# A fixed table of order and engines in place of a list scheduler, in an attention, FFT and feed-forward kernel

## The chip, the cores and the metric

The kernel runs on one core of a Trainium2 chip. The metric is the device time in microseconds of one execution; below 5 us (0.5%) two kernels can't be told apart here. A core has TensorE (PE in the rows, its weight loads PEld), VectorE (DVE), ScalarE (ACT), GpSimd (POOL) and SyncE (SP), which issues nearly all DMAs. Each engine runs its own queue strictly in order, and an instruction whose input isn't there holds up everything behind it on that engine.

## The reference

```python
def reference(**kwargs):
    ...
    attn_out = _attn_ref(**attn_kwargs)      # sliding window of 64, 8 heads of 64
    B, H, S, D = attn_out.shape              # 8, 8, 576, 64
    x = np.ascontiguousarray(attn_out.transpose(0, 2, 1, 3)).reshape(B, S, H * D)
    return _moe_ref(x=x, **moe_kwargs)

def _moe_ref(x, w_ch1, w_ch2):
    X = np.fft.fft(x, axis=1)
    X = np.fft.fft(X, axis=2)
    u = x + np.real(X).astype(np.float32)
    ...
    un = (u - mu) / np.sqrt(var + 1e-06)
    ch = np.maximum(un @ w_ch1, 0.0) @ w_ch2     # 512 x 2048 and 2048 x 512
    return (u + ch).astype(np.float32)
```

Attention over 8 batches of 576 positions, a two-dimensional Fourier transform of its output whose real part is added to it, a normalisation, and a feed-forward net of 2048 hidden units with a residual. The two weight matrices arrive as 64-bit floats.

## The kernel before

**Tiles.** The 4608 positions are 36 tiles of 128 (T0 to T35; nine tiles are a pair of batches). A tile's attention is: load k, q, v (L434); bring k and q into head-major form (L471 for T0 to T12, DMA transposes later); scores (`psc`, L573 or L578); masking and row maximum on VectorE (L595); exponential on ScalarE (L603); transposing the probabilities (`pp`, L614) and copying them out of PSUM; times v (`pa`, L657); division on VectorE (L663 to L667); a radix-4 step for the transform (`y`, L414) and its transposition (`py`, L748). When a batch's tiles are done, `fft` does the rest of its transform: folds and sums on VectorE or GpSimd (L414, L832), splitting each into two f16 halves (`fs`, `hs`), two stages of matmuls (`pg` L888, `pz` L922), and a mix that goes through DRAM (`md`, `mt`). `norm_tile` adds and normalises, giving `uhl`.

**Feed-forward.** 18 chunks of two tiles, c0 to c17. In each, 16 steps `one(f)` (`ph`, L1208, fed by the first weights) and 16 steps `second(f)` (`po`, L1189, fed by the second). Two `one` steps share a PSUM bank; ScalarE (L1217) and then VectorE (L1220) turn it into `hh`, which two `second` steps read. There are two such banks and two `hh` buffers. c0 is the plain case (L1214) in f32; the others are three f16 passes over split weights. The feed-forward work fills TensorE wherever attention and transform leave it free.

**Weights.** 32 pieces of 512 KB (`weight_piece`): 16 of the first matrix (x0, g0 to g15) and 16 of the second (x1), in alternating fours. Each is loaded by SP (L1088), converted by three VectorE steps (L1097, L1102, L1109), and squared on ScalarE (L1115) for a scale. After the last piece of a matrix its scale is known, and `weight_split` (L1162 and a copy) makes the f16 halves for c1 on. Step `one(f)` of c0 needs four converted pieces:

```python
bws = [Bw[0][4 * (f // 4) + kc + at] for kc in range(4)]
op("PE", 1.73 if plain else 1.31, 1e6 + 32 * c + 2 * f, lambda f=f, one=one: one(f), [Bu[c], *bws], [bph])
```

so f12 to f15 need x0 g12 to g15.

**Order.** All 2900 operations are registered with `plan.op` (engine, planned duration, priority, reads, writes; `alt` names a second engine) and numbered as they come. `Plan.order` (L199) is a list scheduler over planned times: it repeatedly picks, of all engines, the operation that can start first, by priority where two tie, and lets an engine wait a little for a more urgent one (`PATIENT`). Of an operation with two engines it takes the second when that finishes sooner by a margin:

```python
sooner = max(free[e2], s2) + d2 + o.margin < max(free[e1], s1) + d1
...
key = (st, o.prio, o.idx)
```

The instructions are then issued in that order (L1278 on, under `manual_schedule`), so the list fixes each engine's queue and SP's queue of DMAs. Where the planner sees TensorE idle before the feed-forward starts, it puts in warm-up matmuls (L1284). An elementwise step on GpSimd is cut in pieces (`both`, L410):

```python
w = out.shape[1] // n if eng is nc.gpsimd else out.shape[1]
for k in range(0, out.shape[1], w):
    eng.tensor_tensor(out=out[:, k : k + w], in0=in0[:, k : k + w], in1=in1[:, k : k + w], op=al)
```

**Numbers that the prediction uses.** Tile T9: 673 scores, 674 and 678 masking of its two head groups, 675 and 679 exponentials, 676 and 680 `pp`, 682 and 684 `pa`. T10: 698 scores. Pieces x0 g12 to g15: conversions 132 to 134, 137 to 139, 142 to 144, 147 to 149. Transform of batch 1: folds 586 and 587, sums and splits 588 to 607, matmul stage 608 and 611. c0: `one(12)` is 397, `second(8)` to `second(11)` are 395, 396, 400, 401. Loads of T4: 271 (k), 272 (q), 273 (v); of T5: 487 to 489; loads of x0 g2, g3 and x1 g0: 21, 26, 31.

Of the kernel before, what the change touches and what calls it, by code (L numbers as in the profile page):

```python
# [53 lines left out]
YS = 32.0  # L54
PASSES = ((0, 0), (0, 1), (1, 0))
ONE = ((0, 0),)


D0, D2, DO1, DO2 = (0, 65), (65, 64), (129, 128), (257, 128)
# [73 lines left out]
class Plan:  # L133
# [3 lines left out]

    SEM = {"PE": 0.22, "DVE": 0.06, "ACT": 0.06, "POOL": 0.08, "DMA": 0.0}
    MARGIN = 0.4
    PATIENT = {"DVE": 0.25, "ACT": 0.5, "POOL": 0.75, "DMA": 0}  # L140
    SELF = {"PE": 0.05, "DVE": 0.02, "ACT": 0.02, "POOL": 0.03, "DMA": 0.0}

    FIXED = {"PE": 0.0, "DVE": 0.1, "ACT": 0.1, "POOL": 0.06, "DMA": 0.0}
# [52 lines left out]
            t += span  # L196
        return t

    def order(self):  # L199
        busy = {}  # L200
        engs = sorted({e for o in self.ops for e in o.durs})
        free = {e: 0.0 for e in engs}
        avail = {e: [] for e in engs}
        slots = {r: [0.0] * n for r, n in self.rings.items()}
        for o in self.ops:
            o.wait, o.ready = len(o.deps), 0.0
            for d in o.deps:
                d.outs.append(o)
        for o in self.ops:
            if not o.wait:  # L210
                for e in o.durs:
                    avail[e].append(o)
        line = {r: [] for r in self.fifo}
        for o in self.ops:
            for b in o.allocs:
                if b.ring in line:
                    line[b.ring].append(((o.prio, o.idx), o))
        for r in line:
            line[r] = [o for _, o in sorted(line[r], key=lambda x: x[0])][::-1]
        port = 0.0  # L220
        res = []
        n = len(self.ops)
        while len(res) < n:
            best = None
            for e in engs:
                t0 = free[e]
                pick, ahead = None, []
                for o in avail[e]:
                    r = o.ready
                    need = {}  # L230
                    for b in o.allocs:
                        need[b.ring] = need.get(b.ring, 0) + 1
                    ok = True
                    for ring, k in need.items():
                        if len(slots[ring]) < k or (ring in line and line[ring][-1] is not o):
                            ok = False
                            break
                        r = max(r, sorted(slots[ring])[k - 1])
                    if not ok:
                        continue  # L240
                    st = max(t0, r, port) if e == "POOL" or e == "DVE" and o.port else max(t0, r)
                    if len(o.durs) > 1:
                        (e1, d1), (e2, d2) = o.durs.items()
                        s1, s2 = (max(port, r) if x == "POOL" or x == "DVE" and o.port else r for x in (e1, e2))
                        sooner = max(free[e2], s2) + d2 + o.margin < max(free[e1], s1) + d1
                        if e != (e2 if sooner else e1):
                            continue
                    key = (st, o.prio, o.idx)
                    ahead.append((o.prio, key, o))
                    if pick is None or key < pick[0]:  # L250
                        pick = (key, o)
                if pick and e in self.PATIENT:

                    most = pick[0][0] + self.PATIENT[e] * pick[1].durs[e]
                    for pr, key, o in ahead:
                        if pr < pick[1].prio and key[0] < most and (pr, key) < (pick[1].prio, pick[0]):
                            pick = (key, o)
                if pick and (best is None or pick[0] < best[0]):
                    best = (*pick, e)
            if best is None:  # L260
                raise RuntimeError("the rings are too small for this order")
            (st, _, _), o, o.eng = best
            o.dur = o.durs[o.eng]
            for e in o.durs:
                avail[e].remove(o)
            gap = st - free[o.eng]
            self.gaps.append(gap)
            end = st + o.dur
            if o.eng == "PE":
                if gap > WARM[0] and o.prio < 1e6:  # L270
                    self.pe_time(busy, free["PE"], (gap - WARM[1]) / 2)
                end = self.pe_time(busy, st, o.dur)
            free[o.eng] = end
            if o.eng == "POOL" or o.eng == "DVE" and o.port:
                port = end
            done = end + o.lat
            for b in o.allocs:
                s_ = sorted(slots[b.ring])
                slots[b.ring] = s_[1:]
                if b.ring in line:  # L280
                    line[b.ring].pop()
            for b in o.bufs:
                b.left -= 1
                b.free_at = max(b.free_at, done + self.SEM[o.eng])
                if b.ring and b.left == 0:
                    slots[b.ring].append(b.free_at)
            for x in o.outs:
                x.wait -= 1
                late = x.slack * self.LATE[o.eng] if "PE" in x.durs else 0.0
                x.ready = max(x.ready, done + (self.SEM if o.eng not in x.durs or o.lat else self.SELF)[o.eng] + late)  # L290
                if not x.wait:
                    for e in x.durs:
                        avail[e].append(x)
            res.append((st, o))
        self.span = max(free.values())
        self.times = [st for st, _ in res]
        return [o for _, o in res]
# [3 lines left out]
def attn_fft_ffn_kernel(ctx: ExitStack, tc: tile.TileContext, q, k, v, w1, w2, gidx, dft_d, dft_s, mask, out):  # L301
# [14 lines left out]
    plan = Plan(RINGS, ("kq", "pr", "pt", "xu", "y", "yT", "tail", "xe", "r3", "fh", "g", "mp", "f1", "f2", "hh"))  # L316
# [754 lines left out]
    osc = cp.tile([P, 1], F32, name="osc")  # L1071

    def weight_piece(x, g, order):

        w, more = {}, order % 7 - 4 if order % 7 > 3 else None
# [41 lines left out]
        bj, bf = Buf("un"), Bw[x][g + 1]  # L1117
        bw = [Buf("big")] if more is None else Bfl[2 * more : 2 * more + 2]
        op("DMA", 1.75, W_DMA + W_DMA_STEP * order, load, writes=[*bw, Bwl], lat=2.5)
        pr = W_CONV + W_STEP * order  # L1120
        op("DVE", 0.34, pr, lambda: conv(0), bw, [bf])
        op("DVE", 0.6, pr - 0.1, lambda: conv(1), bw, [bf])
        op("DVE", 0.6, pr - 0.2, lambda: conv(2), bw, [bf])
        op("ACT", 0.72, W_SQ + W_STEP * order, square, [bf], [bj, Bssq[x]])

    def weight_scale(x, prio):
# [126 lines left out]
    for T in range(NTT):  # L1253
# [5 lines left out]
        pb, n = divmod(T, NT)  # L1259
# [16 lines left out]
    warm = bank("f1", "warm", (P, 2, CH))[:, 0]  # L1276
    early = True
    with tc.manual_schedule():  # L1278
        for o, gap in zip(plan.order(), plan.gaps):
            early = early and o.prio < 1e6  # L1280
            if early and o.eng == "PE" and gap > WARM[0]:

                for _ in range(int((gap - WARM[1]) / 0.21)):
                    nc.tensor.matmul(warm, wide[:, 0:P], wide, start=True, stop=True)  # L1284
            if len(o.durs) > 1:
                o.fn({"DVE": nc.vector, "POOL": nc.gpsimd, "ACT": nc.scalar}[o.eng])
            else:
                o.fn()
# [27 lines left out]
```

## Time and profile before

| what | value |
|---|---|
| median of 3 runs | 1000.35 us (998.46 to 1002.23) |
| profiled execution | 1000.41 us; span from first to last instruction 998.6 us |
| TensorE busy | 964.4 us (97%) |
| VectorE, ScalarE, GpSimd busy | 655.8, 394.2, 254.3 us |
| granted TensorE clock, mean | 0.989 |
| DMA | 123.08 MB |

A busy time is a union: overlapping instructions count once. TensorE's warm-up matmuls count as busy. "1.00" in a clock column is 2.4 GHz, "0.50" is 1.2 GHz. A wait is named by the instruction that ended it.

### The profile page before, as it was taken

How to read it: one execution, taken by the hardware profiler on the slowest of the kernel's cores; microseconds unless marked ns; L12 is line 12 of the kernel's file. 1: busy time of each engine (PE TensorE's matmuls, PEld its weight loads, DVE VectorE, ACT ScalarE, POOL GpSimd, SP SyncE). 2: the span in 40 equal slices, each digit the busy share in tenths (PEclk: the TensorE clock that was granted, in tenths of full speed). 3: DMA queues.
4: the chain of work that ended last, by engine and by line, in shares of the span. 5: the costliest groups of instructions: out<-in, count | busy, mean ns of one | idle time of the engine just before them, and what ended most of it. 6: DMA issues, size and time to landing. Idle time of an engine off the chain costs nothing.

```text
span 998.6 us, 22725 instructions
## 1 busy us (share of the span) xinstructions
PE 964.4 (97%) x8984; PEld 676.3 (68%) x8984; DVE 655.8 (66%) x1846; ACT 394.2 (39%) x893; POOL 254.3 (25%) x500
## 2 busy tenths in 40 slices
PE   7789969999999999999999999999999999999998
PEld 5576638767676667666676667766676677666664
DVE  5699998987875777775885678665867464511111
ACT  5564646762553444344442344233523121211010
POOL 0011100345245521252215254342404101400000
PEclk9899989999999999999999999999999999999999
DMA  9987663435965876888866777568636302410000
GB/s 195 233 216 214 186 167 119 99 67 119 173 156 132 165 153 141 158 168 174 155 124 154 130 150 135 116 133 165 111 86 120 75 1 68 74 32 22 1 22 21
DMA packets 309066, 123.08 MB, mean 123 GB/s; under 512 B 291096, under 2 KB 291224, under 8 KB 308960
## 3 DMA queue, kind: packets, MB, share of 16 engines
q1 hardware_dynamic: 306240, 112.72, 52.2%
q0 software_dynamic: 2720, 8.92, 3.4%
q8 instruction: 70, 1.15, 0.5%
q14 instruction: 36, 0.29, 0.1%
HBM read 54.99 MB, written 14.17 MB: 69 GB/s over the span
## 4 chain that ended last, share of the span: by engine, by line
PE 79%; DMA 8%; DVE 7%; POOL 2%; ACT 1%; SPq 1%; issue 1%; DVEq 0%; ACTq 0%; POOLq 0%
PE ph L1208 33%; PE po L1189 32%; PE pa L657 3%; DMA mt<-md,gix 3%; PE pz L922 3%; PE pg L888 2%; PE psc L578 2%; DMA kn<-in_k 1%; DMA pt<-flex 1%; DMA md<-mp 1%; POOL flex L414 1%; PE pp L614 1%; PE psc L573 1%; DMA qn<-in_q 1%; PE py L748 1%
## 5 line engine op out<-in xcount | busy, mean ns | idle before, releaser
L1208 PE MATMUL ph<-uhl,w0s 128*128 128x256 f16 (+1 forms) x3384 | 425.8, 277 | 0.3 <-DVE hh L1220 0.3
L1189 PE MATMUL po<-w1s,hh 128*128 128x512 f16 (+1 forms) x1696 | 426.0, 388 | 0.0
L1208 PEld LDWEIGHTS <-w0s 128*128 128x128 f16 x3264 | 316.5, 98 | 83.1 <-issue 1.9
L1189 PEld LDWEIGHTS <-hh 128*128 128x128 f16 x1632 | 155.7, 98 | 138.0
L1220 DVE SCALAR_TENSOR_TENSOR hh<-ph,hh 128x512 f16<-128x512 f32 x136 | 93.7, 689 | 156.7 <-ACT hh L1217 156.5
L1217 ACT ACTIVATE hh<-ph 128x512 f16<-128x512 f32 x136 | 81.0, 595 | 283.6 <-PE po L1189 212.1
L603 ACT ACTIVATE pr<-pr,nm 128x128 f32<-128x128 f32 x288 | 91.1, 390 | 26.8 <-DVE nm L595 26.7
L595 DVE CUSTOM_DVE_ANT_0 pr<-psc,mskb 128x128 f32<-128x128 f32 x288 | 65.8, 284 | 16.0 <-PE psc L573 11.4
L414 POOL TENSOR_TENSOR up<-un,up 128x128 f16<-128x128 f32 x128 | 55.4, 461 | 69.4 <-ACT up L404 69.4
L414 POOL TENSOR_TENSOR flex<-pr,flex 128x128 f16<-128x128 f32 x92 | 44.9, 516 | 96.9 <-ACT flex L404 79.3
L996 POOL DMA_INDIRECT mt<-md,gix x34 | 35.7, 1051 | 111.6 <-DMA md<-mp 103.5
L1020 POOL TENSOR_TENSOR rs<-mv,mhalf 128x1 f32<-128x1 f32 x36 | 23.2, 644 | 133.2 <-DVE mv L1016 126.7
L414 POOL TENSOR_TENSOR flex<-qn,flex 128x128 f16<-128x128 f32 x88 | 42.6, 518 | 47.4 <-ACT flex L404 34.8
L657 PE MATMUL pa<-ve,pt 128*64 128x65 f16 (+1 forms) x760 | 43.5, 206 | 3.6 <-DMA pt<-flex 2.3
L657 PE MATMUL pa<-va,pt 128*64 128x65 f16 (+1 forms) x760 | 43.6, 207 | 0.0
L1243 DVE SCALAR_TENSOR_TENSOR xu<-po,osc,xu 128x512 f32<-128x512 f32 x34 | 23.9, 745 | 22.6 <-PE po L1189 22.6
L404 ACT CAST up<-un 128x512 f16<-128x512 f32 x34 | 21.0, 616 | 43.7 <-DMA uhl<-up 14.4
L404 ACT CAST flex<-pr 128x512 f16<-128x512 f32 x40 | 24.6, 616 | 25.4 <-DMA pt<-flex 25.3
L667 DVE TENSOR_TENSOR xu<-pa,rc 128x256 f32<-128x256 f32 x72 | 30.6, 425 | 3.1 <-DMA out<-xu 0.7
L657 PEld LDWEIGHTS <-pt 128*64 128x64 f16 x1104 | 21.1, 111 | 16.7 <-issue 12.2
L922 PE MATMUL pz<-g,ds__75 97*96 97x257 f16 (+3 forms) x240 | 29.1, 273 | 1.0 <-DVE g L898 0.7
L614 PE MATMUL pp<-ident,pr 128*128 128x128 f32 x104 | 19.1, 299 | 9.9 <-ACT pr L603 9.9
(153 smaller groups left out, 1099.6 us busy)
## 6 DMA issues: line engine op xcount, KB each, us to landing
wd<-in_moe_w_ch SPq DMA_DIRECT2D x20, 512.0 KB, 4.2
out<-xu SPq DMA_DIRECT2D x36, 256.0 KB, 2.4
ve<-va SPq DMA_DIRECT2D x67, 130.0 KB, 2.4
kn<-in_k SPq DMA_DIRECT2D x32, 256.0 KB, 3.4
qn<-in_q SPq DMA_DIRECT2D x32, 256.0 KB, 3.7
flex<-in_moe_w_ch SPq DMA_DIRECT2D x12, 512.0 KB, 5.5
flex<-in_v SPq DMA_DIRECT2D x20, 256.0 KB, 4.0
md<-mp SPq DMA_DIRECT2D x24, 192.0 KB, 2.1
```

Of the source, the lines that this page charges most:

```text
L404: nc.scalar.mul(out, in_, scale) if scale is not None else nc.scalar.copy(out, in_)
L414: eng.tensor_tensor(out=out[:, k : k + w], in0=in0[:, k : k + w], in1=in1[:, k : k + w], op=al)
L595: nc.vector.tensor_tensor_reduce(out=t["pr", g][:, hp], in0=t["ps", g][:, hp], in1=mskb[:, m : m + P], scale=-0.125, scalar=3.0e38, op0=AL ...
L603: nc.scalar.activation(pr, pr, AF.Exp, bias=t["nm", g][:, hp : hp + 1], scale=-1.0)
L657: nc.tensor.matmul(pa[sl, hp], pt[:, sl], v_, start=(x == 0), stop=(x == len(mm) - 1))
L667: nc.vector.tensor_tensor(out=xv[:, g::2], in0=pa[:, :, 0:64], in1=rc.to_broadcast([P, 4, 64]), op=ALU.mult)
L922: nc.tensor.matmul(pz[:M, c0:c1], ds_[:NJ, a, c[0] : c[0] + c[1]], t["g", gi][:, b_, c0:c1], start=(x == 0), stop=(x == len(mm) - 1),)
L996: nc.gpsimd.indirect_dma_start(out=mts[T], out_offset=None, in_=mds[pb][0 : HR if n < 4 else 2 * HR], in_offset=bass.IndirectOffsetOnAxis( ...
L1189: nc.tensor.matmul(t["po"][i], l_, r_, start=(f == 0 and x == 0), stop=(f == NKF - 1 and x == len(mm) - 1))
L1208: nc.tensor.matmul(ph, l_, r_, start=(x == 0), stop=(x == len(mm) - 1))
L1217: nc.scalar.activation(t["hh", j][:, 0], ph, AF.Relu)
L1220: nc.vector.scalar_tensor_tensor(out=hh[:, 1], in0=ph, scalar=0.0, in1=hh[:, 0], op0=ALU.max, op1=ALU.subtract)
```

## The change

`Plan.order` is gone. Two tables take its place: `ORDER`, all 2900 numbers in the order of issue, and `SECOND`, the 204 numbers that run on their second engine. `Plan.follow` goes through the table, keeps the planned times (they now only decide the number of warm-up matmuls) and returns the list. No operation is added, dropped or resized; the dependencies, buffers and helper code are as they were.

```diff
+ORDER = [int(i) for i in """
+171 10 0 8 172 1 7 9 4 3 173 174 175 196 176 177 197 180 181 179 178 199 185 182 198 200 201 186 183 222 202 184 187
...
+253 19 241 271 256 20 260 257 26 276 22 277 258 23 219 5 242 220 259 243 261 273 264 274 265 254 262 275 31 27 263 280
+24 244 6 281 266 245 282 487 267 268 25 283 278 36 284 285 269 270 28 490 286 488 298 491 299 287 489 289 288 312 290
...
+110 580 718 122 123 561 671 673 693 365 715 124 366 581 90 392 367 582 131 115 678 583 391 674 679 127 584 128 393 585
+129 120 136 586 125 680 388 130 588 394 132 589 719 389 133 675 395 134 141 590 681 587 396 592 691 591 137 596 400
+593 594 138 135 146 598 401 142 139 672 740 143 140 676 597 602 144 677 151 603 720 682 147 145 684 148 698 739 149
+595 683 150 397 697 599 368 413 600 414 398 604 415 152 716 153 154 742 402 605 699 156 685 700 416 611 417 686 423
...
+""".split()]
+SECOND = {int(i) for i in """
+177 193 200 202 234 238 259 268 293 303 307 312 315 319 321 360 559 595 601 605 607 641 648 655 686 711 713 736 761
...
+""".split()}
...
-    PATIENT = {"DVE": 0.25, "ACT": 0.5, "POOL": 0.75, "DMA": 0}
...
-    def order(self):
...
+    def follow(self, ids, second):
+
+        assert sorted(ids) == list(range(len(self.ops)))
+        busy, done, seen = {}, {}, set()
+        free = {e: 0.0 for o in self.ops for e in o.durs}
         slots = {r: [0.0] * n for r, n in self.rings.items()}
...
+        for i in ids:
+            o = self.ops[i]
+            assert all(d.idx in seen for d in o.deps)
+            e = o.eng = list(o.durs)[i in second]
+            o.dur = o.durs[e]
+            st = free[e]
+            late = o.slack if e == "PE" else 0.0
...
             self.gaps.append(gap)
...
-        for o, gap in zip(plan.order(), plan.gaps):
+        for o, gap in zip(plan.follow(ORDER, SECOND), plan.gaps):
```

Steps of `both` that ran on VectorE in the trace of before and stand in the table for GpSimd, up to operation 607: radix-4 of T1, T2, T6 and T8 (218, 243, 534, 583, whose first engine is GpSimd and which are not in `SECOND`), one f16 split of T3 (367, likewise), five steps of batch 0's transform (307, 312, 315, 319, 321) and four of batch 1's (595, 601, 605, 607). The other way goes radix-4 of T9 (686); four copies out of PSUM go from ScalarE to VectorE (177, 234, 238, 259).

## Rows read from the trace of the kernel before

**Rows 1.** the page, part 1: busy time of each engine.

```profile
PE 964.4 (97%) x8984; PEld 676.3 (68%) x8984; DVE 655.8 (66%) x1846; ACT 394.2 (39%) x893; POOL 254.3 (25%) x500
```

**Rows 2.** busy time by stretch: length, then busy us (instructions) per engine, clock, DMA.

```profile
50.00:100.00 50.00, 44.90 (x442) 34.98 (x437) 46.59 (x131) 28.77 (x77) 7.42 (x15) 1.00 0.77 216
100.00:150.00 50.00, 40.12 (x273) 26.02 (x272) 46.68 (x128) 26.16 (x66) 2.59 (x3) 0.91 0.64 177
...
800.00:960.00 160.00, 160.00 (x1165) 110.34 (x1163) 55.07 (x106) 27.48 (x54) 16.46 (x30) 1.00 0.13 31
```

**Rows 3.** what TensorE waited for, whole span: total us, times, longest.

```profile
PE pp L614 <- ACT pr L603: 9.9, 1, 9.9
PE pk L471 <- DMA kn<-in_k: 5.8, 2, 3.7
```

**Rows 4.** timeline of TensorE, 126 to 156 us (start, length).

```profile
126.70 0.60 PE L614 MATMUL pp<-ident,pr 128*128 128x128 f32 x4
...
128.96 0.27 PE L657 MATMUL pa<-ve,pt 128*64 128x65 f32 x1
...
129.58 1.10 PE L573 MATMUL psc<-kst,qbd 64*64 64x128 f32 x32
...
133.31 5.32 PE L1189 MATMUL po<-w1s,hh 128*128 128x512 f32 x12
148.50 1.35 PE L614 MATMUL pp<-ident,pr 128*128 128x128 f32 x4 [9.88 <-ACT pr L603]
...
155.42 1.46 PE L1208 MATMUL ph<-uhl,w0s 128*128 128x256 f32 x6
```

**Rows 5.** timeline of VectorE, 130 to 150 us.

```profile
130.59 0.76 DVE L414 TENSOR_TENSOR y<-xu 128x256 f32<-128x256 f32 x2
...
131.79 0.42 DVE L1097 TENSOR_SCALAR w1s<-wd 128x512 int32<-128x512 int32 x1
...
139.99 0.56 DVE L414 TENSOR_TENSOR f<-f,xe 128x388 f32<-128x388 f32 x1
...
147.72 0.28 DVE L595 CUSTOM_DVE_ANT_0 pr<-psc,mskb 128x128 f32<-128x128 f32 x1
...
149.75 0.74 DVE L1109 SCALAR_TENSOR_TENSOR wf<-flex,wf 128x512 uint16<-128x512 uint32 x1
```

**Rows 6.** stretches just after two idle times of TensorE (columns as in rows 2).

```profile
43.30:48.60 5.30, 5.22 (x35) 4.68 (x36) 2.89 (x14) 2.93 (x7) 0.00 (x0) 0.50 1.11 246
...
148.50:154.40 5.90, 5.84 (x56) 5.14 (x58) 5.76 (x21) 3.74 (x12) 0.10 (x1) 0.50 0.39 113
```

**Rows 7.** waits of all engines before 200 us.

```profile
DVE w0s L1097 <- DMA wd<-in_moe_w_ch: 3.6, 4, 2.3
```

**Rows 8.** timeline of GpSimd, two stretches.

```profile
49.07 2.46 POOL L414 TENSOR_TENSOR f<-xe 128x97 f32<-128x97 f32 x4 [46.07 <-DVE xe L414]
...
177.90 2.59 POOL L414 TENSOR_TENSOR y<-xu 128x128 f32<-128x128 f32 x4 [0.28 <-DVE s L1143]
180.46 1.44 POOL L414 TENSOR_TENSOR y<-y 128x128 f32<-128x128 f32 x2
```

**Rows 9.** VectorE beside those GpSimd steps, and its L1162 by line (min/median/max).

```profile
49.90 0.75 DVE L414 TENSOR_TENSOR f<-xe 128x388 f32<-128x388 f32 x1
...
178.31 1.02 DVE L1162 SCALAR_TENSOR_TENSOR w0s<-w0s,s 128x512 f16<-128x512 f32 x1
...
180.11 0.93 DVE L1162 SCALAR_TENSOR_TENSOR w0s<-w0s,s 128x512 f16<-128x512 f32 x1
...
L1162 DVE SCALAR_TENSOR_TENSOR w1s<-w1s,s x16: 741/752/939, 179.2 to 217.0; 128x512 f16<-128x512 f32 x16
```

**Rows 10.** the two halves of a feed-forward step: L1217 and L1220, and idle before.

```profile
L1220 DVE SCALAR_TENSOR_TENSOR hh<-ph,hh 128x512 f16<-128x512 f32 x136 | 93.7, 689 | 156.7 <-ACT hh L1217 156.5
L1217 ACT ACTIVATE hh<-ph 128x512 f16<-128x512 f32 x136 | 81.0, 595 | 283.6 <-PE po L1189 212.1
```

**Rows 11.** timeline of TensorE: one step of c1 on, 12 matmuls.

```profile
346.12 1.47 PE L1208 MATMUL ph<-uhl,w0s 128*128 128x256 f16 x12
```

More of the change, by code (lines that the diff above doesn't have):

```diff
@@ L197, in pe_time @@
         return t
-    def order(self):
[L200 to L203, printed above, removed]
-        slots = {r: [0.0] * n for r, n in self.rings.items()}
[L205 to L219, printed above, removed]
+    def follow(self, ids, second):
+        assert sorted(ids) == list(range(len(self.ops)))
+        busy, done, seen = {}, {}, set()
+        free = {e: 0.0 for o in self.ops for e in o.durs}
+        slots = {r: [0.0] * n for r, n in self.rings.items()}
@@ L220, in order @@
         port = 0.0
         res = []
[L222 to L266, printed above, removed]
@@ new lines, in follow @@
+        for i in ids:
[5 more added lines that the diff above has]
+            late = o.slack if e == "PE" else 0.0
+            for d in o.deps:
+                after = (self.SEM if d.eng not in o.durs or d.lat else self.SELF)[d.eng]
+                st = max(st, done[d.idx] + after + late * self.LATE[d.eng])
+            shared = e == "POOL" or e == "DVE" and o.port
+            if shared:
+                st = max(st, port)
+            for b in o.allocs:
+                slots[b.ring].sort()
+                st = max(st, slots[b.ring].pop(0))
+            gap = st - free[e]
@@ L267, in order @@
             self.gaps.append(gap)
             end = st + o.dur
-            if o.eng == "PE":
+            if e == "PE":
                 if gap > WARM[0] and o.prio < 1e6:
@@ L272, in order @@
                 end = self.pe_time(busy, st, o.dur)
-            free[o.eng] = end
-            if o.eng == "POOL" or o.eng == "DVE" and o.port:
+            free[e] = end
+            if shared:
                 port = end
[L276 to L281, printed above, removed]
+            done[i] = end + o.lat
+            seen.add(i)
             for b in o.bufs:
                 b.left -= 1
-                b.free_at = max(b.free_at, done + self.SEM[o.eng])
+                b.free_at = max(b.free_at, done[i] + self.SEM[e])
                 if b.ring and b.left == 0:
                     slots[b.ring].append(b.free_at)
[L287 to L293, printed above, removed]
             res.append((st, o))
```

117 rows, old and new, of tables (ORDER, SECOND) are left out of this document.

## The prediction

> **What bounds the kernel now.** I read the busy times first, then the stretches, then what TensorE waited for, then the three engines' timelines around its longest wait. TensorE is busy 964.4 us of a span of 998.6 [rows 1]; VectorE is next with 655.8. So an order can win at most the 34.2 us in which TensorE does nothing, and what it loses at the lower clock. The stretches say where that is: from 800 to 960 us there is no idle time at all, while 50 to 100 and 100 to 150 miss 5.1 and 9.9 us [rows 2]. In these two VectorE is busy 46.6 and 46.7 us of 50: while the weights are converted, VectorE is the bound and TensorE runs out of feed-forward work of c0.
>
> One wait stands for most of it: `pp` waited 9.9 us, once, for an exponential [rows 3]. The scores of T9 left TensorE at 129.58 + 1.10 = 130.7; TensorE then did `second(8)` to `second(11)` and stood from 138.6 to 148.5 [rows 4]. The scores were ready all that time, but VectorE took up their masking only at 147.72 [rows 5]: in its queue stood the transform of batch 1 and the conversions of x0 g12 to g14 first. A wait made by the order alone. It costs more than its length: the clock is 1.2 GHz for 5.9 us after it, and for 5.3 us after the 3.7 us wait for k [rows 3, 6].
>
> **The change, part by part.**
>
> *The masking of T9 moves up.* In the table 678 and 674 stand ahead of the folds 586 and 587 and of x0 g12's conversions, some 30 VectorE operations earlier. So both `pp` and both `pa` of T9 and the scores of T10 stand ahead of `one(12)` (397) in TensorE's queue, and no transform stage. Their time: `pp` 0.44 (126.70 to the next at 127.14, by its 0.60 less the overlap), `pa` 0.62 (128.96 to 129.58), scores 1.03 (1.10 less overlap) [rows 4]: 2 x 0.44 + 2 x 0.62 + 1.03 = 3.15 us. TensorE then comes to 397 at about 138.6 + 3.2 = 141.8.
>
> *Then 397 waits.* It needs x0 g15, converted at 149.75 + 0.74 = 150.5 [rows 5]; nothing in the table gets around that. So the question is how much earlier VectorE gets there. Queued behind 397 on TensorE are the weight scale, `one(13)` and all of c1.
>
> *VectorE's queue ahead of x0 g15.* Taken out, among steps that fall in its full time after 50 us: radix-4 of T6 and T8 (1.20 each, 130.59 to 131.79), one f16 split (as a transform step, 0.6), five transform steps of batch 0 and one of batch 1 (0.56 each), and three more of batch 1 that the table puts later (599, 600, 601). Put in: one masking of T9 (four pieces of 0.28 less their overlap, 0.85) and one split (603, 0.56) [rows 5]. 2.4 + 0.6 + 3.4 + 1.7 - 1.4 = 6.7 us. Radix-4 of T1 and T2 and the four copies lie before 50 us, where VectorE isn't full; I cost them at nothing, and their cover is its idle time there.
>
> *The price on GpSimd.* These steps become 2 x 6 + 6 x 4 + 4 = 40 pieces on GpSimd. Where the trace has both at work, VectorE slows: beside the six pieces at 177.90 three L1162 take 1.02 (the first) to 0.93 (the last) for a median of 0.75, together about 0.65 us, or 0.11 a piece; beside the four pieces at 49.07 one sum takes 0.75 for 0.56, or 0.05 a piece [rows 5, 8, 9]. So 2.0 to 4.3 us go back; I take the middle, 3.0, as these steps are of both kinds. Net 3.7 us: x0 g15 at 146.8. The Trainium skill (SBUF — State Buffer, Who interferes with whom) states that a VectorE step with two SBUF inputs and a GpSimd step that reads SBUF exclude each other, the later one blocking in full. By that rule the moves would cost more than they save; it is the third rival. The trace so far shows both engines slowed, VectorE by far less than the GpSimd time beside it.
>
> *DMAs.* All loads stay, on SP's one queue. Weights move up against attention loads: 21 and 26 stand ahead of more of T4, 31 ahead of 487. VectorE waited 3.6 us for x0 pieces [rows 7]; between none and all of that can go; I take half, 1.8: x0 g15 at 145.0. Against it k of T4 and T5 come later. Bounds: nothing, and the 3.7 us of the longest wait for k [rows 3]. I cost it at nothing, because up to 150 us the path through TensorE has the rest of the 9.9 us wait as cover; beyond 3 us it would be late itself.
>
> *Sum.* Before, `one(12)` ran at 155.42, with two transform stages behind it that the table puts later (148.50 to 155.42 is 6.9 us, of it 5.9 at half clock, so 4.0 at full; less 0.9 for `pp` and 0.6 for `pa` 2.4), and without one `pa` and the scores of T10 (1.65). So the table is behind by 0.75 when it reaches 397. 155.4 - 145.0 - 0.75 = 9.7 us earlier. TensorE still stands from 141.8 to 145.0, 3.2 us, about as long as the wait for k, so I charge the slow clock again: 5.9 us at half rate, 2.95 [rows 6]. Gain 6.7 us. Against the profiled execution's 1000.41 (the median is 1000.35, the same) that is **993.7**.
>
> *From 200 us on* the table shuffles neighbours on every engine. There is little to win: TensorE is full. Counted over both orders, the TensorE work between a pair's later `one` step and its `second` pair is never under 5 us from c8 on before; in the table it falls in places to two steps of 1.3 us (1.47 less overlap), 2.6 us [rows 11]. The chain under it is 0.595 on ScalarE and 0.689 on VectorE [rows 10], 1.3 us and the hand-overs, so it fits if neither engine is taken. I cost it at nothing; the cover is one more us, and the second rival is that cover gone. Where nobody else uses these engines, 800 to 960 us, the old order shows that TensorE stays full [rows 2]. Warm-up matmuls can change in number; they stand in idle time before c0, and I cost them at nothing too.
>
> **The rivals.**
>
> 1. *No relief* (about the same). GpSimd's slowing eats all of the 6.7 us and the loads bring nothing, so 397 waits to 150.5. For: VectorE is full there, and every piece it hands over is shared. Against: 0.05 to 0.11 us a piece. 155.4 - 150.5 - 0.75 - 2.95 = 1.2 us: 999.2.
> 2. *Thin leads* (slower). In c1 to c13 some 12 of the 104 `second` pairs have a lead under 4 us in the table, two before. If ScalarE or VectorE is in a longer step when the bank is full (a radix-4, 1.2; a masking, 0.85 [rows 5]), 1.3 becomes 3.4 and a pair waits about 0.8 us. It decides from 1.3 us of queue on. For: ScalarE's half waited mostly for a free `hh` (212.1 of 283.6 us, behind L1189), so slots are scarce [rows 10]. Against: VectorE's half waited on ScalarE's alone. 12 x 0.8 = 9.6 us; with the transform's and attention's own short leads, half as much again, 14.4, against the gain of 6.7: 1008.1.
> 3. *The port* (slower). If every GpSimd piece holds VectorE for its length, 0.67 us (2.59 + 1.44 for six [rows 8]), or for half of it, the rest being its own wait, 40 pieces cost 13 to 27 us; with the middle, 20, less 6.7 saved and 1.8 of loads, x0 g15 comes at 162.0, and 155.4 - 162.0 - 0.75 - 2.95 = -10.3: 1010.7. Against it: six pieces in 4.0 us lengthened VectorE's steps by 0.65 us, not by 2 to 4 [rows 9]. The rule of the Trainium skill named above (SBUF — State Buffer, Who interferes with whom) speaks for it.
> 4. *The wait goes whole* (faster). If loads and conversions come early enough that 397 finds its weights, 155.4 - 141.8 - 0.75 = 12.9: 987.5. For: the idle time of VectorE before 50 us. Against: its queue is full from there on.
>
> That the table isn't followed can hardly be: the loop asserts each number once. The planned times it keeps decide only warm-ups.
>
> **How the numbers follow.** The forecast (991 to 996.5) gets 0.46, the whole gain 0.12, no relief 0.24, thin leads 0.11, the port 0.07. The range takes in the fourth rival in part and the first with some waits: 987 to 1004, and leaves out most of the slow cases. Faster by over 0.5% (under 995.4): 0.12 and most of the forecast, 0.40, is 0.52. Within 0.5%: the rest of the forecast and no relief, 0.30. Slower: 0.18.
>
> **What would show it.** Right: no wait of `pp` for L603 near 10 us; instead TensorE waits a few us, ahead of `ph` with x0 g15 (`wf`), for L1109; masking of T9 within 3 us of its scores; more GpSimd time before 150 us; the last L1109 on `wf` near 145. Wrong: that L1109 at 150 or later; waits of `po` for L1220 or of `pa`, `pz` summed over 5 us after 200 us; or a new wait for k of T4 or T5 that pushes c0's first `ph` back by over 3 us.

## The result, and the profile after

| | before | changed |
|---|---|---|
| median of 5 runs | 1002.13 us | 993.26 us (990.80 to 994.33) |
| ratio | | 0.992, 95% interval 0.990 to 0.994 |
| profiled execution; span | 1000.41; 998.6 us | 990.80; 988.6 us |
| first `ph` of c0 | 87.28 us | 83.08 us |
| x0 g15 converted (last L1109, now L1184, on `wf`) | 150.48 us | 140.50 us |
| TensorE at half clock between 100 and 200 us | 13.7 us, 5.9 of it after the long wait | none |

The change is faster by 8.9 us by the medians (5.8 to 10.3 by the interval). The profiled execution of the changed kernel is the fastest of its five; between the two profiled executions the gain is 9.6 us. Lines of the kernel have moved down by 75 (L1208 is L1283, L1189 is L1264, L614 is L689).

Part 1 of the page, after, answers to [rows 1]:

```profile
PE 964.2 (98%) x8964; PEld 672.2 (68%) x8964; DVE 644.1 (65%) x1827; ACT 367.1 (37%) x853; POOL 332.3 (34%) x675
```

TensorE has the same busy time in a shorter span. GpSimd took 78 us more, VectorE and ScalarE gave 39 us up. The stretches, after, with the columns of [rows 2] and [rows 6]:

```profile
50.00:100.00 50.00, 47.51 (x468) 35.54 (x461) 48.30 (x147) 28.67 (x80) 19.63 (x35) 1.00 0.88 236
100.00:150.00 50.00, 47.49 (x342) 33.49 (x341) 42.92 (x126) 29.61 (x80) 16.20 (x25) 1.00 0.64 167
...
148.50:154.40 5.90, 5.90 (x51) 4.59 (x49) 4.90 (x15) 3.98 (x10) 1.36 (x4) 1.00 0.49 139
```

From 100 to 150 us TensorE works 7.4 us more than before, and VectorE, which was full there, has 7 us to spare. The stretch behind the old long wait runs at full clock: with the wait went the clock that it cost. What TensorE waited for, after, largest first and then those that answer to [rows 3]:

```profile
PE pk L546 <- DMA kn<-in_k: 2.9, 3, 1.8
PE pq L546 <- DVE rc L738: 2.4, 1, 2.4
...
PE ph L1283 <- DVE hh L1295: 1.1, 2, 0.8
...
PE pp L689 <- ACT pr L678: 0.9, 2, 0.6
```

The 9.9 us of `pp` are 0.9, and no wait of `ph` for a conversion (L1184) is in the list. TensorE's timeline from `second(8)` to `one(12)` (started with x0 g12 at 141.48, on `wf`, the piece x0 g15, from 142.88) answers to [rows 4]:

```profile
131.12 7.13 PE L1264 MATMUL po<-w1s,hh 128*128 128x512 f32 x16 [0.25 <-ACT hh L1289]
138.09 0.60 PE L689 MATMUL pp<-ident,pr 128*128 128x128 f32 x4
...
140.44 1.10 PE L648 MATMUL psc<-kst,qbd 64*64 64x128 f32 x32
141.48 1.56 PE L1283 MATMUL ph<-uhl,w0s 128*128 128x256 f32 x6
142.88 0.59 PE L1283 MATMUL ph<-uhl,wf 128*128 128x256 f32 x2
```

VectorE's timeline, after, answers to [rows 5]:

```profile
122.38 0.28 DVE L670 CUSTOM_DVE_ANT_0 pr<-psc,mskb 128x128 f32<-128x128 f32 x1
...
127.21 1.36 DVE L489 TENSOR_TENSOR xe<-yT 128x1156 f32<-128x1156 f32 x1 [0.78 <-ACT yT L479]
128.60 0.56 DVE L489 TENSOR_TENSOR f<-xe 128x388 f32<-128x388 f32 x1
129.09 0.42 DVE L1172 TENSOR_SCALAR w0s<-wd 128x512 int32<-128x512 int32 x1
...
139.68 0.82 DVE L1184 SCALAR_TENSOR_TENSOR wf<-flex,wf 128x512 uint16<-128x512 uint32 x1
```

The masking of T9 is done 25 us earlier than before. The conversion ends at 139.68 + 0.82 = 140.50, 0.98 us before TensorE starts `one(12)`, and 2.38 us before it needs that piece. The step at 129.09 begins 0.07 us before the one at 128.60 has ended; the one at 128.60, which reads the `xe` just written, begins 0.03 us after its predecessor's end. That difference comes up again below.

**Where the gain stands.** For each execution I added up TensorE's useful work started by a given time: each matmul counts the median distance to the next of its own kind in the trace of before, warm-ups count nothing. The lead is the difference to before, in us. At 160 and 300 us it moves by some 1 us with how the short matmuls of attention and transform are counted (11.8 to 13.2 for the changed kernel at 160), so smaller differences in these two columns say nothing.

| kernel | at 88 | 138 | 160 | 300 | 500 | 960 |
|---|---|---|---|---|---|---|
| changed | 4.1 | 0.9 | 13.0 | 10.3 | 12.6 | 10.0 |
| order alone | 3.7 | 1.3 | 13.4 | 4.8 | 6.9 | 0.8 |
| engines alone | -2.6 | -5.6 | -6.2 | -11.2 | -18.5 | -37.0 |
| new table with early engines of before | 2.2 | 0.0 | 11.6 | 8.2 | 10.5 | 7.5 |
| order, and 18 norm engines | 1.9 | 0.0 | 11.4 | 6.2 | 7.2 | 3.5 |
| new up to 170 us | 2.2 | -0.9 | 11.0 | 7.6 | 3.7 | 3.4 |
| new from 180 us | -1.3 | -1.7 | -1.9 | -7.9 | -6.2 | -9.7 |
| new up to 88 us | 1.9 | 0.4 | 1.7 | 1.7 | -1.9 | -1.9 |
| new from 88 us | -0.2 | -4.3 | 7.5 | 6.6 | 8.8 | 6.6 |
| changed, fewer switches | 3.9 | 0.9 | 12.6 | 12.3 | 16.5 | 14.0 |

So the changed kernel makes 13 us by 160 us, nearly all of it between 138 and 160, where the kernel before stood, and gives some 3 back after that. Three questions follow: which part of the change makes the 13 us, what keeps it later, and where the 3 us go.

### The profile page after: what moved, and what is told of

Same layout as the page of the kernel before. It is cut to its first block, busy times and chain, and to the rows that moved or that the text cites. A ratio compares the mean times of both kernels' runs of the same rounds, so it can differ in the third digit from the quotient of the medians.

```text
span 988.6 us, 22785 instructions
## 1 busy us (share of the span) xinstructions
PE 964.2 (98%) x8964; PEld 672.2 (68%) x8964; DVE 644.1 (65%) x1827; ACT 367.1 (37%) x853; POOL 332.3 (34%) x675
## 4 chain that ended last, share of the span: by engine, by line
PE 85%; DMA 6%; DVE 5%; ACT 2%; issue 1%; POOL 1%; SPq 0%; DVEq 0%; POOLq 0%; ACTq 0%
PE ph L1283 36%; PE po L1264 35%; PE pa L732 3%; PE psc L653 2%; PE pz L997 2%; PE pg L963 2%; DMA kn<-in_k 2%; PE psc L648 1%; DMA mt<-md,gix 1%; DMA uhl<-up 1%; DMA qbd<-flex 1%; PE pp L689 1%; PE py L823 1%; PE mt L1040 1%; PE warm L1359 1%
## 5 line engine op out<-in xcount | busy, mean ns | idle before, releaser
L1264 PE MATMUL po<-w1s,hh 128*128 128x512 f16 (+1 forms) x1696 | 426.2, 388 | 1.5 <-ACT hh L1289 0.9
L1283 PE MATMUL ph<-uhl,w0s 128*128 128x256 f16 (+1 forms) x3384 | 424.1, 277 | 1.9 <-DVE hh L1295 1.1
L1283 PEld LDWEIGHTS <-w0s 128*128 128x128 f16 x3264 | 316.5, 98 | 81.2 <-issue 3.5
L1264 PEld LDWEIGHTS <-hh 128*128 128x128 f16 x1632 | 154.5, 98 | 139.6 <-DVE hh L1295 1.0
L489 POOL TENSOR_TENSOR flex<-pr,flex 128x128 f16<-128x128 f32 x112 | 49.9, 476 | 54.8 <-ACT flex L479 44.9
L489 POOL TENSOR_TENSOR up<-un,up 128x128 f16<-128x128 f32 x80 | 36.4, 485 | 47.8 <-ACT up L479 36.4
L489 POOL TENSOR_TENSOR flex<-qn,flex 128x128 f16<-128x128 f32 x80 | 36.5, 491 | 28.6 <-ACT flex L479 24.8
L489 POOL TENSOR_TENSOR flex<-kn,flex 128x128 f16<-128x128 f32 x60 | 27.9, 494 | 48.8 <-ACT flex L479 30.4
L479 ACT CAST up<-un 128x512 f16<-128x512 f32 x29 | 17.8, 615 | 48.3 <-DVE un L1099 19.3
L489 POOL TENSOR_TENSOR y<-xu 128x128 f32<-128x128 f32 x36 | 19.3, 568 | 44.8 <-DVE xu L742 39.6
L489 POOL TENSOR_TENSOR hs<-h,hs 128x97 f16<-128x97 f32 x56 | 21.4, 415 | 37.5 <-ACT hs L479 32.2
L653 PEld LDWEIGHTS <-qbd 128*64 128x64 f16 x736 | 21.9, 110 | 13.8 <-issue 13.7
```

Source lines behind the costliest of these rows:

```text
L653: nc.tensor.matmul(out, qbd[i][:, jj, h, 64 * z : 64 * z + 64], keys(h, jj), start=(z == 0), stop=(z == 1))
L1264: nc.tensor.matmul(t["po"][i], l_, r_, start=(f == 0 and x == 0), stop=(f == NKF - 1 and x == len(mm) - 1))
L1283: nc.tensor.matmul(ph, l_, r_, start=(x == 0), stop=(x == len(mm) - 1))
```

## The experiments

Twelve kernels, all with the changed kernel's loop and another table, each timed beside the kernel before. Ratios are to before; where two experiments are compared, each is first set against the before timed beside it. Line numbers differ by a few between them, as the tables have other lengths.

### Order and engines apart

Order alone: the 182 steps on which the two kernels differ go back to the engine they had. With these the planner puts in 98 warm-up matmuls, for 80 in the changed kernel and 100 before.

```diff
 ORDER = (as changed)
-SECOND = {177, 193, 200, 202, 234, 238, 259, 268, 293, 303, 307, 312, ...}   # 204
+SECOND = {193, 200, 202, 218, 243, 268, 293, 303, 360, 367, 451, 479, ...}   # 120, as before
```

> The new order with the engine choices of before: 182 steps go back to the engine that they had. Theory (the end is set by the time at which the weight piece x0 g15 is converted on VectorE, and the change brought that to 140.5 us with two thirds of it from work taken off VectorE): VectorE gets 6.6 us of steps back ahead of that conversion and loses 1.7 us of slowing beside GpSimd, so the conversion ends near 145.4 us, TensorE, which is there at 142.9, waits some 3 us and pays some 3 us at half clock: 999 us. Rival 1 (the order alone made the gain, through the masking of tile 9 moved ahead): 993 us, the conversion still near 141. Rival 2 (the engine choices alone made it): 1002 us, with the conversion near 150.

Measured: 1001.10 us, ratio 1.000 (0.998 to 1.002). The total says that nothing was gained; the stretches say something else. Three views of this kernel: VectorE's timeline, what TensorE waited for, and TensorE's timeline at the longest wait.

```profile
139.84 0.74 DVE L1185 SCALAR_TENSOR_TENSOR wf<-flex,wf 128x512 uint16<-128x512 uint32 x1
```

```profile
PE ph L1284 <- DVE hh L1296: 4.7, 3, 2.7
PE ph L1284 <- DMA uhl<-up: 3.8, 1, 3.8
```

```profile
217.78 8.24 PE L1284 MATMUL ph<-uhl,w0s 128*128 128x256 f16 x48 [3.79 <-DMA uhl<-up]
```

x0 g15 is converted at 140.58, as in the changed kernel, with none of its moves to GpSimd, and the lead at 160 us is 13.4. Then it is lost: TensorE waits 3.8 us for c2's input at 214, runs 6.8 us at half clock behind that, and waits for `hh`. The theory had neither the time nor the conversion right. The total is that of rival 2, and the stretch that decides is that of rival 1: up to 160 us the order alone makes the gain.

Engines alone: the order of before with the new choices.

```diff
-ORDER = [171, 10, 0, 8, 172, 1, 7, ...]
+ORDER = (the order that the list scheduler gave before)
 SECOND = (as changed)
```

> The order of before with the new engine choices. Theory (VectorE's queue ahead of the conversions): with 6.6 us less on VectorE the masking of tile 9 ends 5 to 8 us earlier though it is still behind the batch-1 transform, so the 9.9 us wait of TensorE shrinks to 2 to 5 us: 995 to 997 us, and after 200 us nothing is lost. Rival 1 (the order made the gain): 1002 us, the wait for the masking still over 8 us. Rival 2 (engine choices fit only the order that they were found with): steps stand on GpSimd in places where TensorE waits for them, new waits after 200 us, 1004 us or more.

Measured: 1028.25 us, 1.026 (1.024 to 1.029). The profiled execution took 1037.34, the longest of six and 9 us over the median, so its waits and its loss in the table may be larger than usual. TensorE's waits in it:

```profile
PE pp L694 <- ACT pr L683: 9.1, 1, 9.1
PE py L828 <- POOL y L494: 7.2, 4, 2.2
PE pg L968 <- POOL hs L494: 6.4, 7, 2.3
...
PE ph L1288 <- DVE hh L1300: 4.8, 4, 2.2
```

The wait for T9's masking is hardly shorter (9.1 for 9.9), although VectorE has less to do, and x0 g15 is converted at 157.16, later than before; and TensorE now waits for radix-4 steps and f16 halves that stand on GpSimd. In the changed kernel, with the same engine choices, the first of these is 0.7 us and no wait for `hs` on GpSimd is listed: there the order has such a step ready. This is rival 2, with 24 us more than it had said.

### The engine choices before 170 us

```diff
-SECOND holds 177 234 238 259 307 312 315 319 321 595 601 605 607 686
+SECOND holds 218 243 367 534 583 609 in their place (20 choices as before)
 ORDER, the other choices, the warm-ups: as changed
```

> The new table whole, but the 20 engine choices of the steps planned before 170 us go back to those of before (fewer steps on GpSimd there); same warm-ups. Theory (up to 160 us the order alone makes the gain, the steps given to GpSimd there trade work of VectorE for waits of VectorE): as the changed kernel, 993 us, the last conversion of the piece x0 g15 at 140 to 141 us. Rival 1 (the relief by GpSimd makes a good part of the gain): 997 us or more, that conversion after 144 us. Rival 2 (GpSimd's work slows VectorE, so that taking it away pays): 990 us or less.

Measured: 992.92 us, 0.991 (0.989 to 0.993), the time of the changed kernel. The moves of work to GpSimd before 170 us are worth nothing. VectorE's own account up to the conversion of x0 g15 says why (busy is the union of its records, and the rest is idle, short gaps between neighbours included):

| | converted | busy | idle |
|---|---|---|---|
| before | 150.48 | 123.3 | 27.2 |
| changed | 140.50 | 115.5 | 25.0 |
| order alone | 140.58 | 118.4 | 22.2 |

GpSimd takes 2.9 us of busy time off VectorE, and VectorE stands idle 2.8 us longer. The order by itself removes almost no work (the steps sum up to 142.8 us for 143.2 before), but neighbours overlap more (24.4 us for 19.9), and VectorE stands 5.0 us less. In this experiment the conversion ended at 142.15; c0 began at 84.93, 1.6 us behind order alone. The next one has the same early table and stands like it. These two have fewer warm-ups than order alone, but that need not be the reason: the changed kernel and the runs "fewer switches", "new up to 170 us" and "new up to 88 us" have the same table, engines and warm-ups up to 88 us, and begin c0 at 83.08, 83.27, 84.93 and 85.10. So some 2 us of the lead at 160 us are the spread between executions.

What the two engines cost each other falls mostly on GpSimd. In the changed kernel its 56 steps beside VectorE up to 140.5 us were longer than the same steps alone by some 11 us in sum, 6.2 of that in two pieces. GpSimd's timeline at two splits of the same kind in four pieces:

```profile
49.86 1.41 POOL L489 TENSOR_TENSOR fs<-f,fs 128x97 f16<-128x97 f32 x4 [2.86 <-ACT fs L479]
...
134.57 6.45 POOL L489 TENSOR_TENSOR fs<-f,fs 128x97 f16<-128x97 f32 x4 [8.75 <-ACT fs L479]
```

The second ran beside VectorE's steps from 134.26 to 140.38, which follow each other without a gap; its first piece alone took 4.52 us.

### The engine choices after 170 us

18 of them, the f16 halves of the normalisation's result, go with the new order; the other 164 stay as before. The warm-ups are those of the changed kernel, 80 for the 98 of order alone.

```diff
 SECOND (120, as before)
+  and 641 648 655 859 866 872 1322 1537 1544 1550 1551 1785 1792 1985 1986 1993 1999 2006
 ORDER, warm-ups: as changed
```

> The new order with the engine choices of before, but for 18 choices of the normalisation's halves (u_hi, u_lo) after 170 us, which are made on VectorE as in the changed kernel. Theory (the order alone lost what it had gained because u_lo stands on GpSimd late and its upload comes 3.8 us late at 214 us, and in the same way later): at least the 6.6 us lost at 200 to 250 us come back: 992 to 995 us. Rival (the lead after 200 us hangs on the other 160 choices): 997 to 1001 us, with waits for hh of 2 us and more between 500 and 720 us.

Measured: 997.49 us, 0.994 (0.992 to 0.997); against the before timed beside each, order alone was 0.2 us slower and this is 4.7 faster, so 4.9 us came back, not 6.6 or more. This is the rival's range. TensorE's waits:

```profile
PE po L1262 <- DVE hh L1293: 2.4, 2, 1.7
PE ph L1281 <- DVE hh L1293: 2.2, 3, 1.1
...
PE ph L1281 <- DMA uhl<-up: 1.5, 1, 1.5
```

The wait for the upload is 1.5 for 3.8 us, so most of it came from these steps' place off VectorE; the waits for `hh` stay. With the 20 early choices worth nothing, the other 4.6 us (997.5 to 992.9) hang on the 144 choices left, which I did not take further apart.

### Where in time the gain is made

The table was cut: the steps that one table plans before a time, in its order and on its engines, then the rest as the other has it.

```diff
-ORDER, SECOND = new
+ORDER = [i for i in new if planned_new[i] < 170] + [the rest, in the order of before]
+SECOND: each step as in the table that orders it
```

> The new table for the first 641 steps (planned up to 170 us), the order and engines of before for the rest. Theory (all of the gain is made by 160 us, and the shuffled steps after it are worth nothing or cost up to 3 us): 990 to 993 us, TensorE's idle time after 200 us between 2 and 4 us. Rival (the new order of the later steps carries part of the gain): 996 us or more, with TensorE's waits after 200 us grown by 3 us or more.

Measured: 996.06 us, 0.995 (0.994 to 0.997). The lead is there at 160 us (11.0), 3.1 us go at once where the tables meet (the second line), and more between 300 and 500 us (3.3 us of the first):

```profile
PE pa L734 <- DMA pt<-flex: 4.5, 4, 1.3
...
PE po L1266 <- DVE xu L1318: 3.1, 1, 3.1
```

The rival's numbers came out, but the first 3.1 us go at the seam itself, which neither kernel has, and the waits for DMA transposes may come from it too, or from the old order, which has 2.3 us of them in the kernel before; so this does not show that the later order is worth anything by itself. The reverse says more:

```diff
+ORDER = [i for i in old if planned_old[i] < 180] + [the rest, in the new order]
```

> The order and engines of before for the first 635 steps (planned up to 180 us), the new table for the rest. Theory (the gain is all made by 160 us): no faster than the kernel before, 1002 to 1005 us, with the 9.9 us wait for the masking of tile 9 as before. Rival (the new order of the later steps carries part of the gain): 999 us or less.

Measured: 1011.50 us, 1.010 (1.008 to 1.013); the wait of `pp` is there in full (11.2 us in two), 5.5 us are lost at the seam (lead -1.9 to -7.5 between 160 and 200 us), and from there to 960 us the new table loses 2 us more. Neither time that was expected came out, the theory's for the loss at the seam, but the new table gains nothing after 180 us.

Cut at 88 us, where c0 begins:

```diff
+e9:  ORDER = [i for i in old if planned_old[i] < 88] + [the rest, in the new order]
+e11: ORDER = [i for i in new if planned_new[i] < 88] + [the rest, in the order of before]
```

> The order, engines and warm-ups of before for the first 328 steps (planned up to 88 us), the new table for the rest. Theory (the gain comes from the steps between 88 and 160 us, where the queue of VectorE and TensorE's order were changed together; the 4 us of lead that TensorE has at 88 us are eaten up again by 138 us): 994 to 996 us, the conversion of x0 g15 at 141 to 144 us, no wait of 9 us for the masking of tile 9. Rival (the earlier start, by VectorE's shorter waits in the first 62 us, is what counts): 998 us or more.

> The new table for the first 333 steps (planned up to 88 us), the order and engines of before for the rest. Theory (the gain comes from the steps between 88 and 160 us): TensorE starts the transform some 4 us earlier and then waits longer at the masking of tile 9: 999 to 1002 us. Rival (the earlier start counts): 996 us or less, the wait for the masking not over 10 us.

Measured: new from 88 us 994.56 us, 0.993 (0.991 to 0.995); new up to 88 us 998.82 us, 0.997 (0.995 to 0.999), with this wait in the second:

```profile
PE pp L687 <- ACT pr L676: 11.4, 3, 10.3
```

Most of the gain comes from 88 to 160 us, as expected. The earlier start alone gains 3.5 us by the medians; in its profiled execution, the slowest of twelve, it gains nothing and ends in the same wait. And with the old start x0 g15 is converted only at 145.67, later than the 141 to 144 expected, and the lead at 160 us is 7.5, not 13.0. What the first 88 us bring shows in full only when the wait behind them is gone.

### One part of the order alone

T9's masking and exponentials moved ahead of the batch-1 transform, on VectorE and ScalarE, in the kernel before:

```diff
 VectorE:  ... 127 128 129
+674 678
 586 587 132 133 134 588 ...   (674 and 678 taken out further down)
 ScalarE:  ... 130
+675 679
 135 592 594 ...
```

> The kernel before, but the two masking steps of tile 9 and their exponentials stand ahead of the batch-1 transform on VectorE and ScalarE; TensorE's order is untouched. Theory (the whole of VectorE's queue up to the conversion sets TensorE, the masking is only the first step that it waits for): the wait passes on to the next steps that come out of that queue, the transform of batch 1 and the weights: 999 to 1001 us, TensorE's wait for the exponential gone and one for a VectorE or ScalarE step of the transform in its place. Rival (the masking was the blockage): 994 us or less.

Measured: 1002.31 us, 1.000 (0.999 to 1.002). TensorE's waits from 100 to 180 us:

```profile
PE pg L960 <- DVE hs L486: 4.9, 1, 4.9
PE pg L960 <- DVE fs L486: 2.6, 1, 2.6
PE pg L960 <- ACT fs L476: 2.3, 1, 2.3
PE pg L960 <- ACT hs L476: 0.9, 1, 0.9
```

The 9.9 us of `pp` have become 4.9 + 2.6 + 2.3 + 0.9 = 10.7 us of the transform stage behind it, and the time is that of the kernel before. The masking was only the first thing that TensorE asked of a queue that was late as a whole.

Neighbours parted: in VectorE's queue of before, up to x0 g15, a step that reads what the step ahead of it wrote changes places with the next.

```diff
-VectorE: ... 193 210 ... 14 231 ... 24 27 ... 293 307 ...
+VectorE: ... 210 193 ... 231 14 ... 27 24 ... 307 293 ...
```

> The kernel before, but in VectorE's queue up to the conversion of x0 g15 a step that reads its predecessor's result changes places with the next one: 46 of 63 such neighbours are gone, nothing else is changed. Theory (in the trace of before VectorE starts a step that reads its predecessor's result 18 ns after the predecessor's end and another 79 ns before it, so each neighbour parted saves 97 ns): 46 x 0.097 = 4.5 us less in that queue, the masking of tile 9 and the conversion as much earlier, TensorE's wait of 9.9 us down to some 5.4 us: 996.4 us. Rival (the overlap is only in the records and frees nothing): 1000.9 us, the conversion still at 150 us.

Measured: 1002.81 us, 1.000 (0.999 to 1.002), a miss. VectorE's busy time up to the conversion did fall, from 123.3 to 119.1 us (4.2, near the 4.5 expected), but its idle time grew from 27.2 to 34.4 us, 3.2 of that up to the fourth conversion (63.7 us before, 66.1 here). As I read it, the steps that were put back by one place were awaited by others: TensorE's wait in `py` for radix-4 steps on VectorE grew from 1.7 to 4.5 us. The conversion:

```profile
152.73 0.74 DVE L1181 SCALAR_TENSOR_TENSOR wf<-flex,wf 128x512 uint16<-128x512 uint32 x1
```

It ends at 153.47, 3 us later than before. The saving is real; a swap that doesn't look at who waits loses it. The 18 ns of the theory is a mean over 145 neighbours whose names match: 125 of them start 34 ns after their predecessor (median), the other 20 overlap like steps that read something else. So a parted neighbour is worth some 113 ns, not 97.

### Where the 3 us go

Between 175 and 960 us both kernels have the same sum of TensorE's waits over 0.4 us (3.1 us each), though not the same waits. After 200 us the kernel before has these two, and the changed one 2.3 us of `ph` and `po` for `hh` and `uhl`:

```profile
PE pa L657 <- DMA pt<-flex: 2.3, 2, 1.5
PE ph L1208 <- DVE hh L1220: 0.3, 1, 0.3
```

What differs is in the distances between neighbouring matmuls of different kinds. Leaving feed-forward work for `pa` or `psc` costs 93 ns beyond the usual distance. Coming back costs 99 ns: `pa` and `psc` start in pairs, the next pair 29 and 53 ns later, and a feed-forward matmul instead 128 and 152 ns later. To and from `pp`, `py`, `pz` or `pg` it costs nothing. Rows name the difference: `pa` and `psc` are tiles of 128\*64 of the array (a few still 64\*64), the feed-forward and the transposes 128\*128. The kernel before has 143 such switches there, 14.0 us; the changed one 174, 16.7 us. That is 2.7 of the 3 us: the new order cuts attention into smaller portions between feed-forward steps. The Trainium skill (TensorEngine Tiling (Array Packing), Key Properties) states that a change of the tiling mode drains TensorE, without a price; the trace agrees, with 0.1 us each way.

So I moved attention and transform steps in the changed kernel's TensorE queue, after 175 us, by up to six places so that they stand together:

```diff
 TensorE: ... 2025
-707 2030 709 2031 2033 726 ...
+2030 707 709 2031 2033 726 ...
```

> The changed kernel with 74 fewer switches of TensorE between feed-forward matmuls and others (180 for 254 from 175 us on), got by moving steps of attention and transform up to six places in TensorE's queue next to each other; the other queues and the engines stay. Theory (from 175 us on the changed kernel gives back 3.0 us of its lead: 31 more such switches than before, at 0.09 to 0.13 us each by the starts of neighbouring matmuls): 74 x 0.1 = 7 us less, 986 us, or up to 2 us more where a step now comes too late. Rival (a switch costs nothing by itself, the lead is given back in waits): 992 to 995 us, with TensorE's idle time as before or more.

Measured: 987.32 us, 0.986 (0.984 to 0.988), 6 us faster than the changed kernel and 15 faster than before. TensorE's timeline at one place, where 6 matmuls of `po` are followed once by `ph` and once by `pa`:

```profile
354.21 1.46 PE L1265 MATMUL po<-w1s,hh 128*128 128x512 f16 x6
355.50 1.47 PE L1284 MATMUL ph<-uhl,w0s 128*128 128x256 f16 x12
356.81 1.46 PE L1265 MATMUL po<-w1s,hh 128*128 128x512 f16 x6
358.20 0.22 PE L733 MATMUL pa<-ve,pt 128*64 128x65 f16 x1
```

The first six take 355.50 - 354.21 = 1.29 us to the next start, the second 358.20 - 356.81 = 1.39. Of the 74 switches taken out, 59 were between the two tile shapes (174 to 115), and these distances fell from 16.7 to 11.0 us, 0.097 us each. Against that, waits grew by 1.2 us, and between the two profiled executions the gain is 3.9 us, not 6. The largest wait:

```profile
PE ph L1284 <- DVE hh L1296: 3.2, 4, 1.5
```

The same on the kernel before:

```diff
 TensorE: the queue of before after 175 us, 45 places changed, 32 switches fewer
```

> The kernel before with 32 fewer switches of TensorE between feed-forward matmuls and others from 175 us on (190 for 222), got in the same way as in the run with 74 fewer; all else as before. Theory (a switch costs 0.08 to 0.1 us by itself, in either table): 32 x 0.09 = 2.9 us less than before, 999.3 us, with TensorE's idle time before 200 us untouched. Rival (the 6 us of the other run came from that table's own waits): 1002 us.

Measured: 1002.17 us, 1.001 (0.9995 to 1.003), no gain. Of its 32 switches 21 were between the shapes (143 to 122), and their distances fell from 14.0 to 11.7 us, 0.11 each, as the theory has it. New waits took all of it:

```profile
PE pa L729 <- DMA pt<-flex: 1.9, 2, 1.7
PE psc L650 <- DMA qbd<-flex: 1.6, 1, 1.6
PE po L1261 <- DVE xu L1315: 1.2, 1, 1.2
```

Waits over 0.4 us rose from 3.1 to 5.5 us. The price of a switch is the same in both tables; whether it can be saved depends on what the moved step meets.

## Why the prediction was right, and where it was not

The number was right (993.7 for 993.3, a gain of 6.7 inside the measured 5.8 to 10.3), but by luck, through two errors of opposite sign: some 13 us were made where 6.7 were forecast, and some 3 lost where nothing was. The times agree better than the gains (6.7 for 8.9 by the medians) because the median of before is 1.7 us above the execution that the forecast started from.

- *An order can win at most the idle time and the slow clock*: too tight. TensorE's busy time before holds 14.0 us of tile switches between 175 and 960 us, and taking 59 of 174 out of the changed kernel made it 6 us faster, though its waits grew.
- *The masking of T9 moves up*: right as far as it goes. No wait near 10 us is left, the masking starts 1.4 us behind its scores (they end at 120.96), and TensorE came to `one(12)` at 141.48 where 141.8 was worked out from the rows. That this needed the rest of the queue too, T9 alone shows: 1002.3 us.
- *VectorE's queue ahead of x0 g15*: here is the mis-sized term. 145.0 was forecast, 140.5 measured. The 6.7 us of work taken out was right (6.6, each step counted at its median length when GpSimd is idle). The price on GpSimd was too high: 120 VectorE steps ran beside GpSimd, 44 before, and were longer by 2.05 and 0.38 us in sum, so 1.7 us, under the 2.0 to 4.3 given. The loads, or whatever else shortened VectorE's idle time, gave 2.2 us for 1.8. What I had not in the sum at all is that VectorE's neighbours overlap more in the new order (22.9 us for 19.9): 6.6 - 1.7 + 2.2 + 3.0 makes the 10 us. And the cause was misjudged: I put the gain down to relief by GpSimd, but the same conversion comes at 140.6 us with the engines of before. It is the order.
- *397 waits, and the slow clock again*: wrong, as a consequence. The conversion was there 0.98 us before TensorE, so neither the 3.2 us stand nor the 2.95 us of half clock came. Of the signs named for a right forecast, the wait of `ph` on `wf` for L1109 is missing and the conversion is not near 145; of those for a wrong one, none is there. Rival 4, *the wait goes whole*, with a chance of 0.12 and a gain of 12.9, is what happened up to 160 us, where the lead is 13.0.
- *k of T4 and T5*: costed at nothing, and it was better than that. The wait for `kn` fell from 5.8 to 2.9 us, and c0 began 4.2 us earlier.
- *From 200 us on, nothing*: wrong by 3.0 us, and not by the mechanism of rival 2. Thin leads bit little: the waits of `ph` and `po` for `hh` and `uhl` after 200 us rose from 0.3 to 2.3 us, and the 2.3 us that `pa` waited for a transpose before are gone. The loss is in switches of the tile shape, of which the prediction said nothing; all its rows were there in the trace of before. Rival 2's mechanism exists, though. With the engines of before, the same order waits for `hh` and an upload and loses 12.6 us after 160. What I called a shuffle of neighbours has its value in that the engine choices go with it.
- *Rival 3, the port*: refuted. A VectorE step beside GpSimd was longer by 17 ns on average (2.05 us over 120). Even if the 2.8 us of idle time that VectorE has more than with order alone were all delay by GpSimd, the price is under 5 us, not 13 to 27. By the rule of the Trainium skill (SBUF — State Buffer, Who interferes with whom), an exclusive lock by which the later of two such steps blocks in full, VectorE would lose up to the rest of a GpSimd step each time it comes second. The trace does not show that for VectorE. It shows it for GpSimd, whose steps up to 140.5 us became some 11 us longer beside VectorE.
- *Rival 1, no relief*: its premise, that relief by GpSimd is worth nothing, was right, and its time wrong, since the order did without it.

What stays open: which reorderings in the first 88 us shorten VectorE's waits, which of the 144 later engine choices keep the lead, and what makes the 2 us between executions with equal early tables. The clock does not: in the four named above the half clock before 88 us lasted 6.8, 6.8, 3.4 and 6.8 us. TensorE's waits for the loads of k and q before c0 were 3.5, 3.2, 7.7 and 6.4 us, so the landing of these loads goes with it.

## What to carry to other kernels

An order and its engine choices are one thing: alone, the order was worth 0, the engines cost 27 us, together they gave 9. A long wait on one step may tell that a queue is late, not that the step is the cause; see what the waiting engine asks for next before moving it. On a full TensorE, count the changes between full and half-width tiles: 0.1 us each way here, 17 us of the changed kernel, and grouping attention steps brought 6 us where the moved steps still found their inputs.

## What the runs showed of the hardware

- A change between 128\*128 tiles and 128\*64 ones cost TensorE 93 ns going in and 99 ns coming back (medians of 86 and 88 in the changed kernel, 175 to 960 us), with no record of its own: it shows only in the distance of the starts, and counts as busy. A change between f32 or f16 kinds of 128\*128, or to 97\*96, cost none.
- VectorE starts a step that reads nothing from its predecessor 79 ns before the predecessor's recorded end, on average, and one that does 34 ns after it (mean and median of 232 and 125 neighbours less than 60 ns apart, in the trace of before up to 150 us).
- VectorE steps beside GpSimd were longer by 17 ns on average, 2 us in sum for 41 us of shared time up to 140.5 us. GpSimd's steps beside VectorE were longer by some 11 us there; one piece of 0.37 us took 4.52.
